# A convolution by FFT and a soft mixture of experts on one core: first stage in 60 and 30 columns, last stage in 64 and 26 frequencies, and the product in place

## The chip, the cores and the metric

The kernel runs on one NeuronCore of a Trainium2 chip. Its five engines are PE (matmul, with its weight loads shown as PEld), DVE (VectorE), ACT (ScalarE), POOL (GpSimd) and SP, whose queue issues nearly all DMAs here. Each runs its instructions in order. The metric is the device time of one execution in microseconds. All data are float32.

## The reference

```python
def _attn_ref(x, h):                     # x (8, 5696, 128), h (5696, 128)
    L = 2 * S
    Yf = np.fft.rfft(x, n=L, axis=1) * np.fft.rfft(h, n=L, axis=0)[None, :, :]
    return np.fft.irfft(Yf, n=L, axis=1)[:, :S, :]

def _moe_ref(x, phi, w1, w2):            # x (45568, 128), phi (128, 32)
    logits = x @ phi
    d = softmax over the 45568 tokens of logits
    slot_input = (d.T @ x).reshape(8, 4, 128)
    for e in range(8):
        slot_out[e] = np.maximum(slot_input[e] @ w1[e], 0) @ w2[e]   # 128 -> 1024 -> 128
    c = softmax over the 32 slots of logits
    return c @ slot_out                  # (45568, 128)
```

A causal convolution of every sequence with h along the tokens, then a soft mixture over all tokens, which weighs them over the whole batch before the experts can run.

## The kernel before, in words

The transform of a sequence is cut in two: 5,696 tokens are 89 rows of 64 (`N1` = 90 frequencies of the first stage, `N2` = 64 columns n2). It works on nine groups g: g = 0 is h, g = 1 to 8 are the sequences. The rows are mirrored, so sums and differences of two mirrored columns (`fold`, with `comp` 0 and 1) are transformed apart.

- **Stage A**, `stage_a(c, comp)`, one chunk c of 4 + 4 columns per step. `load_x` brings the rows (80 and 9 in two DMAs) into one of three tiles xc. `fold` adds or subtracts the mirrored half on POOL (L201) into xf[0] or xf[1]. Two matmuls by the 128-wide table s1 (L212, real and imaginary part) fill two PSUM banks, ACT copies them into fst (L214), and two DMAs of 45 partitions store them to f in DRAM (L218). The table has its 90 frequencies at columns 6 to 50 and 82 to 126.
- **Stage B**, for each unit u of up to eight frequencies, twelve units per group: `load_g` reads f (L236), `stage_b1` transforms over n2 with 64x64 matmuls into bt in PSUM (L250). DVE multiplies bt by Hr into pr and by Hi into pi (L270), and pr and pi are added and subtracted into yf (L279). The sum is on POOL where `share` is set, which is in steps with t < 27 or t >= 72. For g = 0 the same lines make Hr and Hi (L274, one half on POOL). `stage_b2` transforms back (L294), ACT copies bz to zst (L299), and one DMA stores z (L302).
- **Stage C**, for each of 32 pairs T of chunks: `load_pair` reads z (64 and 26 frequencies in two DMAs, L330) into the one tile zc. `stage_c1` makes four products by i1, each of two 64-column matmuls over 128 partitions (L349): two, then `stage_c4` of an earlier pair, then two more. ACT copies one of each two (L358, L362), DVE adds and subtracts (L354, L355). `after()` then folds the result out into y with four operations on POOL (L368). `stage_c2` transposes y (L377), ACT copies to yt (L379), `stage_c3` makes the logits (L386), `column_max` and `stage_c4` to `stage_c6`, `softmax` and `dispatch` do the softmaxes, the weighted sums over tokens and the storing of the combine weights.

PSUM is a ring of four banks for stages A and C, which `bank()` gives out in turn, and one buffer each for bt and bz.

The order is written out by hand: the pools run under `manual_schedule`, so every engine keeps the order of the program, and the kernel waits only for data and buffers. One loop over steps t places all stages. In step t it does, in this order: `stage_a(t, 0)`; `fold(t+1, 0)`; for even t `dispatch`; a unit of stage B in even t; in odd t `stage_c1` with `stage_c4` inside, in even t `stage_c2` and `stage_c6`; `after()`; in odd t a unit of stage B; `load_pair`; `load_x(t+3)`; in odd t `stage_c5`; `stage_a(t, 1)`; `fold(t+1, 1)`; in even t `stage_c3` and a second unit of stage B; `column_max` and `softmax`. Stage B starts in step 9, stage C in step 27, stage A ends with step 71, and the loop with step 80. So two steps, odd and even, are a period with three units of stage B and one pair of stage C. Behind the loop come the last pairs of stage C, the experts, and the combine with its stores to the output.

Of the kernel before, what the change touches and what calls it, by code (L numbers as in the profile page):

```python
# [10 lines left out]
F32 = mybir.dt.float32  # L11
AF = mybir.ActivationFunctionType
AL = mybir.AluOpType
# [4 lines left out]
def z_blocks(n):  # L18

    return [(0, 64, 32), (64, n - 64, 0)]  # L20


def transform_tables(S, N1, N2, CH, X0, F0, F1):

# [14 lines left out]
    s1 = np.stack([np.cos(a1), -np.sin(a1), -np.cos(a1)], 1)  # L41
    a0 = np.outer(alpha, np.arange(N1 // 2) + 0.5)
    i1 = np.stack([np.cos(a0), -np.sin(a0), -np.cos(a0)], 1)
    NP = N1 // 2
    part = s1
    s1 = np.zeros((P, 3, P))
    for a, p in enumerate((F0, F1)):
        s1[X0:X0 + R1, :, p:p + NP] = part[:, :, a * NP:(a + 1) * NP]
    part = i1[np.arange(N1).reshape(2, NP).T.reshape(-1)]
    i1 = np.zeros((P, 3, N2))  # L50
    for r, n, p in z_blocks(N1):
        i1[p:p + n, :, 0:NP] = part[r:r + n]
# [5 lines left out]
    back = np.arange(N2).reshape(2, HALF // CH, CH).transpose(1, 0, 2).reshape(-1)  # L58
# [5 lines left out]
    for a in range(2):  # L64
        wq[a] = w[a * NP:(a + 1) * NP].transpose(1, 0, 2)
        for q in range(NP):
            vq[q % 2, :, q // 2, a] = w[a * NP + q][back].T
            tn[q % 2, :, 0, q // 4, a, q // 2 % 2] = np.cos(turn[a * NP + q]) / N
            tn[q % 2, :, 1, q // 4, a, q // 2 % 2] = np.sin(turn[a * NP + q]) / N
    wq, vq, tn = [t.reshape(P, *t.shape[2:]) for t in (wq, vq, tn)]  # L70
    return [np.ascontiguousarray(t, dtype=np.float32) for t in (s1, i1, wq, vq, tn)]
# [3 lines left out]
def kernel(  # L75
# [42 lines left out]
    assert S == R1 * N2 and R1 == N1 - 1 and D == P and CH == Q == 4  # L118
    SPLIT = R1 // 16 * 16
    X0, F0, F1 = 20, 6, 82  # L120
    ctx.enter_context(tc.manual_schedule())

    t_s1, t_i1, t_w, t_v, t_turn = [
        nc.inline_tensor(t, f"tab_{n}").ap()
        for n, t in zip(("s1", "i1", "w", "v", "turn"), transform_tables(S, N1, N2, CH, X0, F0, F1))]
    fd = [nc.dram_tensor(f"f_{g}", (2, N2, NP, 2, D), F32, kind="Internal").ap() for g in range(B + 1)]
    zd = [nc.dram_tensor(f"z_{b}", (NP, 2 * N2, 2, D), F32, kind="Internal").ap() for b in range(B)]
# [8 lines left out]
    i1 = const.tile([P, 3, HP], F32, name="i1")  # L136
# [24 lines left out]
    s1 = apool.tile([P, 3, P], F32, name="s1", tag="s1", bufs=1)  # L161
# [12 lines left out]
    xf = [apool.tile([P, CH, D], F32, name=f"x{i}", tag=f"x{i}", bufs=1) for i in range(2)]  # L174
# [4 lines left out]
    def load_x(c):  # L179
        if c >= (B + 1) * NJ:  # L180
            return
        g, j = divmod(c, NJ)
        src = (h if g == 0 else x[g - 1]).rearrange("(a n) d -> a n d", n=N2)
        t_ = xcs[c % len(xcs)]
        gap = N2 - CH * (2 * j + 1)
        for r in (slice(0, SPLIT), slice(SPLIT, R1)):
            v = src[r, CH * j:CH * (j + 1), :]
            v = bass.AP(tensor=v.tensor, offset=v.offset,
                        ap=[v.ap[0], [gap * D, 2], [1, CH * D]])
            nc.sync.dma_start(  # L190
                out=t_[X0 + r.start:X0 + r.stop, :, :, :].rearrange("p s n d -> p s (n d)"), in_=v)
        xs[c] = t_
# [3 lines left out]
    def fold(c, comp):  # L196
# [3 lines left out]
        y_ = xf[comp]  # L200
        nc.gpsimd.tensor_tensor(out=y_[:, :, :], in0=t_[:, 0, :, :], in1=t_[:, 1, ::-1, :],  # L201
                                op=AL.subtract if comp else AL.add)
        folded[(c, comp)] = y_

    def stage_a(c, comp):
        g, j = divmod(c, NJ)
        src = folded.pop((c, comp))
        tab = (0, 1) if comp == 0 else (1, 2)
        st = apool.tile([P, CH, 2, D], F32, name="fst", tag="fst", bufs=5)
        for G in range(2):  # L210
            p = bank()
            nc.tensor.matmul(p[:, :], s1[:, tab[G], :],  # L212
                             src[:, :, :].rearrange("p n d -> p (n d)"), start=True, stop=True)
            nc.scalar.activation(st[:, :, G, :],  # L214
                                 p[:, :].rearrange("p (n d) -> p n d", d=D), AF.Copy)
        n0 = comp * HALF + CH * j
        for a, p in enumerate((F0, F1)):
            nc.sync.dma_start(  # L218
                out=fd[g][a, n0:n0 + CH, :, :, :].rearrange("n q c d -> q n (c d)"),
                in_=st[p:p + NP, :, :, :].rearrange("k n c d -> k n (c d)"))  # L220
# [9 lines left out]
    def load_g(u):  # L230
        if u >= (B + 1) * NW:
# [5 lines left out]
            out=t_[:, 0:n, :, :].rearrange("p q c d -> p (q c d)"),  # L237
            in_=fd[g].rearrange("a r q c d -> (a r) (q c d)")[:, 8 * w * D:(8 * w + 2 * n) * D])
        gs[u] = t_

    def stage_b1(u, share):
# [15 lines left out]
        else:  # L257
            pv = bt[r, :, 0, :].rearrange("p a (c d) -> p a c d", c=2)
        k = 2 * m
        tags = ("yf", "yf") if g == 0 and w % 2 else ("pr", "pi")  # L260
        pr, pi = [bpool.tile([P, 4, 2, D], F32, name="p", tag=x, bufs=2 if x == "yf" else 1)
                  for x in tags]
        for p_, H_ in ((pr, turn[:, 0]), (pi, turn[:, 1])) if g == 0 else ((pr, Hr), (pi, Hi)):
# [6 lines left out]
            nc.vector.tensor_tensor(out=p_[r, 0:k, :, :], in0=pv, in1=h_, op=AL.mult)  # L270
        if g == 0:
            for c, op_, H_, eng in ((0, AL.add, Hr, nc.vector), (1, AL.subtract, Hi, nc.gpsimd)):
                h_ = H_[r, w, :, :, :].rearrange("p a o d -> p (a o) d") if m == 2 else H_[r, w, :, 0, :]
                eng.tensor_tensor(out=h_, in0=pr[r, 0:k, c, :], in1=pi[r, 0:k, 1 - c, :], op=op_)  # L274
            return
        y_ = bpool.tile([P, 4, 2, D], F32, name="yf", tag="yf", bufs=2)
        for c, op_, eng in ((1, AL.add, nc.gpsimd if share else nc.vector),
                            (0, AL.subtract, nc.vector)):
            eng.tensor_tensor(out=y_[r, 0:k, c, :], in0=pr[r, 0:k, c, :],  # L279
                              in1=pi[r, 0:k, 1 - c, :], op=op_)  # L280
        prods[u] = y_

    def stage_b2(u):
# [6 lines left out]
        for o, (i, n) in enumerate(us):  # L290
# [11 lines left out]
        nc.sync.dma_start(  # L302
            out=zd[g - 1][4 * w:4 * w + k, :, :, :].rearrange("q r c d -> r q (c d)"),
            in_=st[:, :, :, :].rearrange("p o q x -> p (o q) x")[:, 0:k, :])
# [4 lines left out]
    zn = used = None  # L309
    ybufs = [ypool.tile([P, Q * CH, D + 1], F32, name=f"y{i}") for i in range(2)]  # L310
    zring = [ypool.tile([P, 2, 2, CH, 2, D], F32, name="zc")]
# [4 lines left out]
    nc.vector.memset(zring[0][:, :, :, :, :, :], 0.0)  # L316
# [5 lines left out]
    def load_pair(T):  # L322
# [5 lines left out]
        w_ = 2 * 2 * CH * 2 * D  # L328
        for r, n, p in z_blocks(N1):
            nc.sync.dma_start(  # L330
                out=t_[p:p + n, :, :, :, :, :].rearrange("k h o n c d -> k (h o n c d)"),
                in_=zd[b].rearrange("q (a r) c d -> (q a) (r c d)",
                                    a=2)[r:r + n, j * w_:(j + 1) * w_])
        zs[T] = t_

    def stage_c1(T, between):
        t_ = zs.pop(T)
        kr = used if t_ is zn else P
# [7 lines left out]
        def product(o, tab, q):  # L346
            p = bank()
            for h_ in range(2):
                nc.tensor.matmul(p[h_ * HP:(h_ + 1) * HP, :], i1[0:kr, tab, :],  # L349
                                 t_[0:kr, h_, o, :, q, :], start=True, stop=True)  # L350
            return p[:, :].rearrange("p (n d) -> p n d", d=D)

# [4 lines left out]
        b_, a_ = product(0, 1, 1), product(0, 0, 0)  # L357
        nc.scalar.activation(part(0, 0), b_, AF.Copy)  # L358
        fold_out(a_, part(0, 0), part(1, 0))
# [506 lines left out]
```

## Time and profile before

| | |
|---|---|
| device time, three runs | 924.53 us median (923.91 to 933.71) |
| span of the profiled execution | 922.1 us, from the first to the last instruction |
| PE, DVE, ACT, POOL busy | 818.0, 653.1, 481.7, 488.1 us |
| DMA | 272.45 MB in 156,552 packets, 295 GB/s over the span |
| mean granted PE clock | 0.943 |

Busy time is the time in which at least one instruction of an engine runs; matmuls are pipelined, so neighbours overlap. L12 is line 12 of the kernel that was profiled. An arrow in a wait names what released it. The profiled execution's own time outside the span is not recorded; the median stands 2.4 us above the span.

### The profile page before, as it was taken

Reading aid. Unit: us, or ns where it says so; the run is one execution under the profiler, and the core shown is the slowest. Engines: PE = TensorE matmul, PEld = TensorE weight load, DVE = VectorE, ACT = ScalarE, POOL = GpSimd, SP = SyncE. Lnnn points to the kernel's source line nnn. Section 1 sums busy time; section 2 is a strip of 40 time slices with the busy share of each in tenths; the row PEclk is TensorE's granted clock in tenths of the full one; section 3 lists DMA queues with packets and bytes.
Section 4 is the critical chain, followed back from the end, with each engine's and each line's share of the span. In section 5 each row is a group of like instructions: output and inputs, shape, how many; then the busy total and the mean of one; then the engine's idle time right before and its main releaser. Section 6 shows DMA issues by size and latency. Waiting matters only on the chain.

```text
span 922.1 us, 19325 instructions
## 1 busy us (share of the span) xinstructions
PE 818.0 (89%) x7220; PEld 423.9 (46%) x7220; DVE 653.1 (71%) x887; ACT 481.7 (52%) x888; POOL 488.1 (53%) x426
## 2 busy tenths in 40 slices
PE   6968898899999999999999999999987777878893
PEld 2323344345444445544554454444444434345783
DVE  3047665478888878888888788988887775674552
ACT  4623454455556655555666666656553344475442
POOL 4648766546655565556565655655466552472000
PEclk9989999899999999999999999999999888798865
DMA  9989999999899999999999999999989887761798
GB/s 298 279 274 299 272 345 311 289 345 327 268 320 319 314 282 324 316 314 285 341 304 327 289 324 329 297 318 320 316 269 330 272 254 198 211 249 73 272 405 341
DMA packets 156552, 272.45 MB, mean 295 GB/s; under 512 B 11766, under 2 KB 114422, under 8 KB 153317
## 3 DMA queue, kind: packets, MB, share of 16 engines
q1 hardware_dynamic: 155883, 270.85, 91.4%
q8 instruction: 58, 0.95, 0.4%
q10 hardware_dynamic: 576, 0.36, 0.2%
q14 instruction: 35, 0.29, 0.1%
HBM read 142.86 MB, written 128.21 MB: 294 GB/s over the span
## 4 chain that ended last, share of the span: by engine, by line
PE 51%; DMA 31%; POOL 5%; DVE 5%; issue 3%; SPq 2%; ACT 2%; DVEq 0%; POOLq 0%; ACTq 0%
PE bank L212 17%; DMA zc<-z 11%; PE bank L349 9%; DMA gt<-f 8%; PE bt L250 7%; PE bz L294 6%; DMA out_dram<-o 4%; PE bank L377 4%; DVE p L270 2%; POOL y L368 2%; DMA f<-fst 2%; PE bank L462 2%; DMA z<-zst 2%; PE bank L438 2%; PE bank L386 2%
## 5 line engine op out<-in xcount | busy, mean ns | idle before, releaser
L212 PE MATMUL bank<-x,s 128*128 128x512 f32 x576 | 275.9, 614 | 12.3 <-POOL x L201 12.0
L201 POOL TENSOR_TENSOR x<-xc 128x512 f32<-128x512 f32 x144 | 192.8, 1342 | 154.7 <-PE bank L212 70.4
L214 ACT ACTIVATE fst<-bank 128x512 f32<-128x512 f32 x288 | 171.9, 597 | 95.5 <-PE bank L212 74.8
L299 ACT ACTIVATE zst<-bz 128x1024 f32<-128x1024 f32 x96 | 93.2, 971 | 205.4 <-PE bz L294 198.5
L270 DVE TENSOR_TENSOR p<-bt,Hr 128x1024 f32<-128x1024 f32 x96 | 112.9, 1176 | 108.0 <-PE bt L250 95.7
L212 PEld LDWEIGHTS bank<-x,s 128*128 128x128 f32 x576 | 102.4, 193 | 131.5 <-issue 93.4
L279 DVE TENSOR_TENSOR yf<-p 128x512 f32<-128x512 f32 (+1 forms) x163 | 146.4, 931 | 3.3
L250 PE MATMUL bt<-gt,wt 64*64 64x256 f32 x1620 | 116.4, 394 | 25.1 <-DMA gt<-f 22.0
L349 PE MATMUL bank<-zc,i 128*64 128x512 f32 x480 | 117.1, 610 | 7.0 <-DMA zc<-z 4.1
L294 PE MATMUL bz<-yf,vt 64*64 64x256 f32 x1440 | 104.9, 393 | 15.5 <-POOL yf L279 15.0
L270 DVE TENSOR_TENSOR p<-bt,Hi 128x1024 f32<-128x1024 f32 x96 | 112.3, 1170 | 0.0
L250 PEld LDWEIGHTS bt<-gt,wt 64*64 64x64 f32 x1620 | 55.0, 134 | 102.0 <-issue 31.6
L368 POOL TENSOR_TENSOR y<-y,op 128x512 f32<-128x512 f32 x64 | 77.5, 1211 | 7.8 <-DVE op L354 5.1
L294 PEld LDWEIGHTS bz<-yf,vt 64*64 64x64 f32 x1440 | 58.2, 137 | 44.2 <-POOL yf L279 21.0
L279 POOL TENSOR_TENSOR yf<-p 128x512 f32<-128x512 f32 (+1 forms) x29 | 45.9, 1583 | 53.9 <-DVE p L270 53.9
L368 POOL TENSOR_TENSOR y<-y,om 128x512 f32<-128x512 f32 x54 | 71.8, 1330 | 2.1
L270 DVE TENSOR_TENSOR p<-bt,turn 128x1024 f32<-128x1024 f32 (+1 forms) x24 | 27.2, 1174 | 57.8 <-PE bt L250 57.7
L349 PEld LDWEIGHTS bank<-zc,i 128*64 128x64 f32 x480 | 30.8, 138 | 68.3 <-issue 40.8
L377 PE MATMUL bank<-ident,y 109*128 109x109 f32 x512 | 60.0, 275 | 0.7 <-DVE y L368 0.7
L377 PEld LDWEIGHTS bank<-ident,y 109*128 109x128 f32 x512 | 53.5, 151 | 13.6 <-issue 11.9
L379 ACT ACTIVATE yt<-bank 128x360 f32<-128x360 f32 x128 | 50.9, 482 | 3.3 <-PE bank L377 3.3
L819 PE MATMUL op<-so,cT 32*128 32x128 f32 x704 | 46.0, 374 | 4.4 <-ACT o L828 3.6
(97 smaller groups left out, 851.5 us busy)
## 6 DMA issues: line engine op xcount, KB each, us to landing
f<-fst SPq DMA_DIRECT2D x288, 180.0 KB
gt<-f SPq DMA_DIRECT2D x99, 512.0 KB
z<-zst SPq DMA_DIRECT2D x88, 512.0 KB
zc<-z SPq DMA_DIRECT2D x30, 1024.0 KB
xc<-in_x_dram SPq DMA_DIRECT2D x64, 320.0 KB
out_dram<-o SPq DMA_DIRECT2D x16, 1024.0 KB
zc<-z SPq DMA_DIRECT2D x30, 416.0 KB
out_dram<-o SPq DMA_DIRECT2D x8, 768.0 KB
```

The source lines that it names most:

```text
L201: nc.gpsimd.tensor_tensor(out=y_[:, :, :], in0=t_[:, 0, :, :], in1=t_[:, 1, ::-1, :], op=AL.subtract if comp else AL.add)
L212: nc.tensor.matmul(p[:, :], s1[:, tab[G], :], src[:, :, :].rearrange("p n d -> p (n d)"), start=True, stop=True)
L214: nc.scalar.activation(st[:, :, G, :], p[:, :].rearrange("p (n d) -> p n d", d=D), AF.Copy)
L250: nc.tensor.matmul(bt[q * HP:(q + 1) * HP, a, o, :], wt[r, 2 * i + q, :], t_[r, 2 * o + q, :, :].rearrange("p c d -> p (c d)"), start=True ...
L270: nc.vector.tensor_tensor(out=p_[r, 0:k, :, :], in0=pv, in1=h_, op=AL.mult)
L279: eng.tensor_tensor(out=y_[r, 0:k, c, :], in0=pr[r, 0:k, c, :], in1=pi[r, 0:k, 1 - c, :], op=op_)
L294: nc.tensor.matmul(bz[a * HP:(a + 1) * HP, q, o, :], vt[r, i, a, :], y_[r, a * m + o, :, :].rearrange("p c d -> p (c d)"), start=True, sto ...
L299: nc.scalar.activation(st[:, 0:m, 0:n, :].rearrange("p o q x -> p q o x"), bz[:, 0:n, 0:m, :], AF.Copy)
L349: nc.tensor.matmul(p[h_ * HP:(h_ + 1) * HP, :], i1[0:kr, tab, :], t_[0:kr, h_, o, :, q, :], start=True, stop=True)
L368: eng.tensor_tensor(out=part_, in0=part(v, 0), in1=o_[:, :, :], op=sign)
L377: nc.tensor.transpose(p[:, i * TR:(i + 1) * TR], ys[T][0:TR, k * CH + i, 0:D], ident[0:TR, 0:TR])
L379: nc.scalar.activation(yt[:, k * CH:(k + 1) * CH, :, :], of_tokens(p), AF.Copy)
```

## The change

- **Stage A.** Both folds of a chunk now stand in one tile, xf is three such tiles, and `stage_a(c, high)` is split by frequency, not by fold. In every step `stage_a(t, False)` makes frequencies 0 to 59 of both folds of chunk t, two 64-column matmuls side by side in each bank. In odd steps, in the place of the former second call, `stage_a(t, True)` makes frequencies 60 to 89 of both folds of chunks t-1 and t, four 32-column matmuls in each bank. There are three evictions per step on average, not four. f is stored frequency by frequency, so a store is one run of 4 KB per partition (60 partitions, or 30), and `load_g` reads runs of 1 KB.
- **The nine last rows** of a load go to partitions 100, 103, ..., 124, not to 100 to 108.
- **Product in place.** Hi's product goes to pi, Hr's back into bt itself; sum and difference read bt and pi, both on DVE; `share` is gone.
- **z.** Its rows are split by the half o of n2, which alternate on the partitions of zst. Frequencies 0 to 63 go to zm by two DMAs, 64 to 89 to zr by four, with real and imaginary part apart (512-byte runs). zr has two buffers, whose padding is zeroed at the start by eight DMAs on ACT's queue.
- **Stage C.** `load_pair` reads zm and zr, 128 partitions each. `stage_c1` makes all four products first: eight 64x64 matmuls over 64 frequencies and eight 32x64 matmuls over 26, which accumulate in four banks. `stage_c4` follows.

The core of the diff (the tables follow it and are left out):

```diff
+        for r, p in ((slice(0, SPLIT), slice(X0, X0 + SPLIT)), (slice(SPLIT, R1), slice(X1, X1 + XSTEP * (R1 - SPLIT - 1) + 1, XSTEP))):
...
-        y_ = xf[comp]
+        y_ = xf[c % len(xf)]
...
+    def stage_a(c, high):
+        st = apool.tile([P, CH, 2, D], F32, name="fst", tag="fst", bufs=4)
+        if high:
+            groups = [(c_, o, HALF, slice(HP, HP + HALF)) for c_ in (c - 1, c) for o in range(2)]
+        else:
+            groups = [(c, o, HP, slice(0, HP)) for o in range(2)]
+        for q in range(2):
+            p = bank()
+            for i, (c_, o, m, cols) in enumerate(groups):
+                nc.tensor.matmul(p[i * m:(i + 1) * m, :], s1[:, q + o, cols], columns(c_, o),
+                                 start=True, stop=True)
             nc.scalar.activation(...)
+        k0, k1 = (LOW, N1) if high else (0, LOW)
+        for i, (c_, o, m, _) in enumerate(groups):
+            n0 = o * HALF + CH * (c_ % NJ)
+            nc.sync.dma_start(
+                out=fd[g][k0:k1, n0:n0 + CH, :, :].rearrange("k n c d -> k (n c d)"),
+                in_=st[i * m:i * m + k1 - k0, :, :, :].rearrange("k n c d -> k (n c d)"))
...
-        for p_, H_ in ((pr, turn[:, 0]), (pi, turn[:, 1])) if g == 0 else ((pr, Hr), (pi, Hi)):
+        for p_, H_ in (((pi[r, 0:k, :, :], turn[:, 1]), (pv, turn[:, 0])) if g == 0 else
+                       ((pi[r, 0:k, :, :], Hi), (pv, Hr))):
...
-        for c, op_, eng in ((1, AL.add, nc.gpsimd if share else nc.vector),
-                            (0, AL.subtract, nc.vector)):
+        for c, op_ in ((1, AL.add), (0, AL.subtract)):
+            nc.vector.tensor_tensor(out=y_[r, 0:k, c, :], in0=pv[:, :, c, :],
+                                    in1=pi[r, 0:k, 1 - c, :], op=op_)
...
+        for o in range(2):
+            if 8 * w < MAIN:
+                nc.sync.dma_start(
+                    out=zm[g - 1][o, 8 * w:8 * w + 2 * k].rearrange("(q a) r c d -> (a r) q (c d)", a=2),
+                    in_=sv[o::2, 0:k, :])
+                continue
+            k0 = 8 * w - MAIN
+            for c in range(2):
+                nc.sync.dma_start(
+                    out=zr[g % 2][o, c, k0:k0 + 2 * k].rearrange("(q a) r d -> (a r) q d", a=2),
+                    in_=sv[o::2, 0:k, c * D:(c + 1) * D])
...
+        ps = {(o, c): bank() for o, c in ((0, 1), (1, 0), (0, 0), (1, 1))}
+        for c in (1, 0):
+            for h_ in range(2):
+                for o in range(2):
+                    r = slice(o * HP, (o + 1) * HP)
+                    nc.tensor.matmul(ps[o, c][h_ * HP:(h_ + 1) * HP, :], im[r, c, :],
+                                     zt[r, h_, :, c, :], start=True, stop=False)
+        for h_ in range(2):
+            for (o, c), p in ps.items():
+                r = slice((2 * o + c) * HALF, (2 * o + c) * HALF + N1 - MAIN)
+                nc.tensor.matmul(p[h_ * HP:(h_ + 1) * HP, :], ir[r, :], zx[r, h_, :, :],
+                                 start=False, stop=True)
...
-            stage_a(t, 0)
+            stage_a(t, False)
             fold(t + 1, 0)
...
-            stage_a(t, 1)
+            if t % 2:
+                stage_a(t, True)
             fold(t + 1, 1)
```

## The prediction, made before the changed kernel ran

> **What bounds the kernel now.** I read the busy line first, then the stretches, then the timeline of one pair of steps, then the waits. PE is busy for 89% of the span and the SP queue's packets fill 91% of the 16 DMA engines, so both look full:
>
> ```profile
> PE 818.0 (89%) x7220; PEld 423.9 (46%) x7220; DVE 653.1 (71%) x887; ACT 481.7 (52%) x888; POOL 488.1 (53%) x426
> q1 hardware_dynamic: 155883, 270.85, 91.4%
> ```
>
> An average hides the stages. By stretches (columns: stretch; busy us and count of PE, PEld, DVE, ACT, POOL; granted clock; DMA share; GB/s), the first is steps 0 to 26, before any last-stage work; the second the 22 pairs of steps in which all stages run, from the first `stage_c1` at 182.6 us to the one at 664.7; the third the four pairs after the first stage has ended:
>
> ```profile
> 0.00:182.60 182.60, 149.15 (x841) 62.85 (x841) 87.21 (x89) 79.61 (x124) 114.92 (x90) 0.96 0.94 295
> 182.60:664.70 482.10, 469.80 (x4146) 234.99 (x4145) 407.14 (x542) 286.70 (x521) 277.02 (x240) 1.00 0.99 313
> 664.70:743.20 78.50, 64.87 (x700) 35.22 (x700) 60.07 (x87) 34.76 (x65) 43.49 (x38) 0.93 0.91 293
> ```
>
> A pair takes 482.1 / 22 = 21.9 us and PE is busy for 97% of it: PE's own work sets the pace, with the DMA engines just as full beside it. The first stretch is DMA's (share 0.94, PE 82%).
>
> The timeline of one pair shows what matters for this change, POOL against PE (columns: start, us, engine, line, operation, count):
>
> ```profile
> 474.07 2.44 POOL L368 TENSOR_TENSOR y<-y,op 128x512 f32<-128x512 f32 x2
> 476.48 2.76 POOL L368 TENSOR_TENSOR y<-y,om 128x512 f32<-128x512 f32 x2
> 479.20 1.71 POOL L201 TENSOR_TENSOR x<-xc 128x512 f32<-128x512 f32 x1
> ...
> 475.42 3.60 PE L212 MATMUL bank<-x,s 128*128 128x512 f32 x8
> 478.95 1.09 PE L462 MATMUL bank<-y,d 128*32 128x129 f32 x32
> ```
>
> The eight passes at 475.42 are the second half of `stage_a` of odd step t and then the first half of step t+1, which starts at 477.14. POOL's `fold(t+1, 1)` runs behind the four L368 operations of `after()` and ends at 480.91, 3.8 us after PE has begun step t+1. Today that costs nothing, since only `stage_a(t+1, 1)`, at 483.89, reads it. The same lateness stands in the other pairs (3.7 to 5.0 us in those from 477 to 654).
>
> **The change, part by part.**
>
> *First stage on PE.* An f32 matmul is two passes. A full-width pass of 512 costs 275.9 us / 576 = 479 ns (L212), a 64-column pass 117.1 / 480 = 244 ns (L349), a 32-column pass 3.64 / 32 = 114 ns (L764). A pair had 16 full passes, 7.7 us. Now the 60 columns take 8 passes of 64 columns in each step (1.95 us) and the 30 columns of both steps 16 passes of 32 columns in the odd step (1.8 us): 5.7 us, a saving of 1.9. ACT's L214 drops from 8 to 6 evictions of 597 ns; nothing waits there.
>
> *Last stage on PE.* `stage_c1` had 16 passes of 244 ns, 3.9 us. Now 16 passes on 64x64 tiles, priced by L250 (16 passes of 256 columns in 0.92 us from start to start, so 1.85 us for 512), and 16 on 32x64 tiles, which no row shows: 0.95 us if eight run at once, 1.85 if four. L819 packs four row groups at 40 ns a pass, near its share, so I take 0.95: 2.8 in all, a saving of 1.1. The Trainium skill (TensorE: Matmul & The Clock Gate, Measured speedup vs the span model) has four row tiles of 512 gain 3.07 rather than 4; by that the 0.95 would be 1.25 and the total 6 us longer. L250's fourfold packing shows no such loss: 58 ns a pass, where a quarter of a full-width pass of 256 columns is 60. The four banks are now taken at once; the two that `stage_a` used last come free by L214, 0.85 us after its end, while the first half of c1 runs.
>
> *In-place product.* Two operations on PSUM at the price of L354 (0.69 us) replace L279 (0.93 mean on DVE, stretched to 1.6 when POOL runs). Where POOL did one of them (L279, 29 times, and L274), DVE now does both. A unit costs DVE 2 x 1.18 + 2 x 0.69 = 3.75 us, three units 11.2, with the rest 18 us per pair. bt is held 1.4 us longer; its next writer comes 4 us later, so nothing waits, unless DVE starts late.
>
> *The new wait.* `stage_a(t+1, False)` reads both folds of step t+1, as the first thing PE does in that step. For odd t the second fold stands on POOL, in the order of the changed program's instructions, behind L431 and the four L368, and PE's second matmul of the step waits for it. Behind that matmul wait all of the step's PE work and then DVE and ACT. I lay out one pair from the end of odd `stage_a`:
> - To the fold: c1 2.8; copy of y with its signal 0.7 (L358, 0.60), since c4's bank is freed by it and all four products now come first; c4 0.7; copy of L 0.65; DVE rm 0.75; POOL L431 with the memset before it 1.35; four L368 at 1.2, the price without DVE beside it, 4.8; fold 1.27, signal 0.1. Sum 13.1.
> - PE's own work meanwhile: c1 2.8, wait for y 0.8, c4 0.6, b1 and b2 1.9, c5 0.5, the 32-column matmuls 1.9. Sum 8.5. PE stands still for 4.6 us, less 1.0 for the step's first matmul, which needs only the first fold.
> - After the fold: `stage_a` 1.9, dispatch 1.0, b1 and b2 1.9, c2 1.6, c6 0.45, wait for yt 0.15, c3 0.75, b1 and b2 1.9, `stage_a` 1.9. Sum 11.55.
>
> A pair: 13.1 + 11.55 = 24.65 us against 21.9, +2.75, over 22 pairs +60 us. The 3.0 us that PE saves is smaller than the 4.6 + 0.8 of new waits.
>
> *The clock.* PE will stand for 3.6 us in each pair. In the third stretch it stands for 2.84 us before L294, and what follows runs at half speed:
>
> ```profile
> 480.89 1.04 PE L294 MATMUL bz<-yf,vt 64*64 64x256 f32 x16
> 715.04 1.98 PE L294 MATMUL bz<-yf,vt 64*64 64x256 f32 x16 [2.84 <-POOL yf L279]
> ```
>
> The clock there is 0.93 over 78.5 us, 5.5 us lost in four pairs, 1.4 each; in the second stretch 1.00. Bounds: 0, as after the shorter waits of the second stretch, to 1.7 in every pair (L294 and the L377 after it lost 0.9 and 0.8). I take 0.85: +19 us. The skill (same page, HAM oscillation) says that a gap longer than its 3.4 us window re-throttles each turn; by it the term would be 37, and it speaks against this change.
>
> *DMA.* The f stores go from 1,024-byte packets to 4,096, the gt loads the other way, 26 of 90 z rows to 512 bytes. In the trace's packet records 1,024 bytes take 46 ns (median) and 4,096 take 159, so f gains what gt loses. z becomes 3 to 8 DMAs per pair, 5 more SP issues of 0.4 us, and `load_pair` moves 1,536 KB, not 1,440, on all 128 partitions. A pair's 6.8 MB in 24.65 us is 276 GB/s, against 313 reached now, so in the second stretch I cost it at nothing; the cover is PE's longer pair, and gone below 276 GB/s. In steps 0 to 26, 27 x 180 f packets of 4,096 gain 25 ns each (4 x 46 - 159) on 16 engines, 7.6 us, the 27 gt loads of 128 such packets lose 5.4, and steps 0 to 8, now 4.0 us apart (L212 at 31.65, 35.76 and 39.76), of which PE 3.7, may gain 0.5 each: -6 us (bounds -15, +8: the 1 KB loads may stretch as the 4 KB ones do, 203 mean to 159 median, and the eight new zero-fills on ACT's queue may hold its first evictions).
>
> *After step 71.* POOL's L279 leaves the chain (it delayed L294 above), but DVE's 18 us then sets a pair of 19.6: about 18.6, -4 us (0 to -6). Then: `stage_c1` is shorter, the first load needs no copy of a gap: -4 (-8 to +3).
>
> **Sum.** 922.1 - 6 + 60 + 19 - 4 - 4 = 987. The median of the runs is 924.53, 2.4 above this span: 989.
>
> **Rivals.**
> - *The fold stays hidden (faster).* One mechanism: the POOL chain from c1 to the fold takes 8.5 us or less, not 13.1, so PE keeps its saving, at 18.9 us a pair, until DMA stops it: 6.7 MB at the best stretch's 321 GB/s is 20.9. 22 x -1.0, and -14 elsewhere: 922 - 36 + 2 = 888. It decides from a chain 2.75 us shorter than I sum (there a pair is as now). For it: POOL is only 53% busy and loses L279. Against: in every pair read the fold is 3.7 us late or more, and nothing moves it ahead of L368.
> - *The gain and the wait cancel (no change).* The chain is 2 to 3 us shorter through a free DVE: 925. Against: only 0.5 us of L368 and 0.45 of the fold are stretched by DVE now, and these are out of my sum.
> - *DMA becomes the bound (slower).* If 1 KB loads and 512-byte stores pull the rate to 250 GB/s, a pair takes 27.2 us: +116, and +10 in the first stretch: 1050. It decides below 276 GB/s. For it: the engines are full now; against: the bytes are the same within 1%.
>
> **How the numbers follow.** The fold wait 0.75 (its own range 950 to 1025: the chain's terms to half a us either way, the clock 0 to 37), fold hidden 0.12, cancelled 0.06, DMA 0.07. A measurement of this kernel tells about 1% from no change. Faster by over 1% 0.12, within 1% 0.06, slower 0.82. The range 930 to 1040 leaves out the hidden fold and half of the DMA case.
>
> **What would show it.** PE's second `stage_a` matmul of even steps waiting for POOL's fold, some 3.6 us, 22 times; pairs of 25 us; PE near 73% and a clock near 0.97 in that stretch, DMA share under 0.95 there; the 32x64 group near 1 us; no POOL wait before b2. The forecast is wrong if pairs are below 22 us, or if PE waits there for DMA instead.

## The result, and the profile after

The changed kernel takes 1,025.89 us (median of four runs, 1,018.48 to 1,029.66), the kernel before 929.12 us beside it (923.91 to 935.97): a ratio of 1.104, with a 95% interval of 1.095 to 1.112. The profiled execution took 1,018.48 us, 1.8 more than its span of 1,016.7; it is the shortest of the four and has the highest mean granted clock (0.911, the others 0.894 to 0.897), so what is read from it below stands 7.4 us under the median.

The page's busy lines and the SP queue's line show that neither of the two full resources is full now:

```profile
PE 788.5 (78%) x8308; PEld 386.1 (38%) x8308; DVE 631.6 (62%) x928; ACT 440.9 (43%) x816; POOL 401.1 (39%) x385
q1 hardware_dynamic: 176287, 273.91, 83.2%
```

The same stretches as before, cut at the first matmul of the same calls of `stage_c1` (columns: stretch; busy us and count of PE, PEld, DVE, ACT, POOL; granted clock; DMA share; GB/s):

```profile
0.00:197.10 197.10, 136.91 (x1052) 49.54 (x1052) 99.23 (x116) 62.84 (x96) 70.38 (x63) 0.90 0.89 274
197.10:771.10 574.00, 467.90 (x4850) 213.00 (x4848) 366.80 (x540) 262.71 (x476) 256.61 (x239) 0.94 0.86 271
771.10:847.50 76.40, 60.50 (x778) 35.55 (x780) 63.99 (x99) 35.01 (x66) 27.39 (x28) 0.93 0.88 289
847.50:1016.70 169.20, 123.22 (x1636) 88.04 (x1628) 101.54 (x176) 80.36 (x178) 46.72 (x55) 0.81 0.71 265
```

The 22 pairs, 482.1 us before, are 574.0: a pair has gone from 21.9 to 26.1 us, +91.9 of the +94.6 in all. Steps 0 to 26 cost 14.5 us more (182.6 before), the four pairs behind step 71 2.1 less, the rest 9.7 less. In the pairs PE has gone from 97% to 82% busy and the DMA share from 0.99 to 0.86: both now wait for something else.

One pair shows it, PE first (columns: start, us, engine, line, operation, tiles, count, and the idle time before with its releaser), then POOL:

```profile
535.08 1.95 PE L374 MATMUL bank<-zc,im 64*64 64x512 f32 x16
536.96 1.11 PE L379 MATMUL bank<-zx,ir 26*64 26x512 f32 x16
...
541.83 2.93 PE L218 MATMUL bank<-x,s 128*32 128x512 f32 x18
548.14 1.93 PE L218 MATMUL bank<-x,s 128*64 128x512 f32 x6 [3.38 <-POOL x L200]
...
560.08 1.95 PE L374 MATMUL bank<-zc,im 64*64 64x512 f32 x16
```

```profile
542.03 2.46 POOL L392 TENSOR_TENSOR y<-y,op 128x512 f32<-128x512 f32 x2
544.44 2.43 POOL L392 TENSOR_TENSOR y<-y,om 128x512 f32<-128x512 f32 x2
546.84 1.25 POOL L200 TENSOR_TENSOR x<-xc 128x512 f32<-128x512 f32 x1
```

PE has done two passes of the even step's `stage_a` and then stands for 3.38 us until 548.14, when POOL's fold (L200) has ended at 548.09 behind the four operations of `after()` (now L392). The waits of PE over all 22 pairs have this as their first line (columns: us in total, times, longest):

```profile
PE bank L218 <- POOL x L200: 72.6, 21, 4.1
PE bank L439 <- ACT y L382: 14.9, 21, 0.7
```

### The profile page after: what moved, and what is told of

It reads as the page before. It is cut to its first block, busy times and chain, and to the rows that moved or that the text cites. A ratio compares the mean times of both kernels' runs of the same rounds, so it can differ in the third digit from the quotient of the medians.

```text
span 1016.7 us, 21393 instructions
## 1 busy us (share of the span) xinstructions
PE 788.5 (78%) x8308; PEld 386.1 (38%) x8308; DVE 631.6 (62%) x928; ACT 440.9 (43%) x816; POOL 401.1 (39%) x385
## 3 DMA queue, kind: packets, MB, share of 16 engines
q8 instruction: 65, 1.06, 0.4%
## 4 chain that ended last, share of the span: by engine, by line
PE 48%; POOL 15%; DMA 13%; ACT 9%; DVE 6%; issue 6%; SPq 2%; POOLq 0%; DVEq 0%; ACTq 0%
PE bank L218 15%; POOL y L392 9%; PE bt L260 9%; PE bz L303 6%; PE bank L374 5%; DMA gt<-f 4%; DMA out_dram<-o 4%; PE bank L486 4%; ACT yt L403 4%; PE bank L379 3%; POOL x L200 3%; ACT zst L308 3%; PE bank L410 2%; POOL L L455 2%; ACT y L382 2%
## 5 line engine op out<-in xcount | busy, mean ns | idle before, releaser
L218 PE MATMUL bank<-x,s 128*32 128x512 f32 (+1 forms) x1152 | 259.9, 654 | 91.5 <-POOL x L200 91.4
L200 POOL TENSOR_TENSOR x<-xc 128x512 f32<-128x512 f32 x144 | 180.3, 1268 | 178.7 <-PE bank L218 88.0
L220 ACT ACTIVATE fst<-bank 128x512 f32<-128x512 f32 x216 | 128.8, 597 | 214.0 <-PE bank L218 181.0
L280 DVE TENSOR_TENSOR pi<-bt,Hi 128x1024 f32<-128x1024 f32 x96 | 112.9, 1176 | 92.6 <-PE bt L260 92.6
L218 PEld LDWEIGHTS bank<-x,s 128*32 128x32 f32 (+1 forms) x1152 | 59.4, 129 | 246.5 <-POOL x L200 121.7
L288 DVE TENSOR_TENSOR yf<-bt,pi 128x512 f32<-128x512 f32 x192 | 119.3, 662 | 3.3
L280 DVE TENSOR_TENSOR bt<-bt,Hr 128x1024 f32<-128x1024 f32 x96 | 113.0, 1177 | 0.0
L303 PE MATMUL bz<-yf,vt 64*64 64x256 f32 x1440 | 108.2, 398 | 0.0
L392 POOL TENSOR_TENSOR y<-y,op 128x512 f32<-128x512 f32 x64 | 77.6, 1212 | 5.4 <-DVE op L366 2.9
L491 DVE SCALAR_TENSOR_TENSOR acc<-acc,dn,bank 128x129 f32<-128x129 f32 x31 | 10.1, 326 | 106.6 <-PE bank L486 106.6
L303 PEld LDWEIGHTS bz<-yf,vt 64*64 64x64 f32 x1440 | 63.1, 141 | 24.1 <-issue 2.2
L392 POOL TENSOR_TENSOR y<-y,om 128x512 f32<-128x512 f32 x54 | 63.7, 1180 | 2.1
L374 PE MATMUL bank<-zc,im 64*64 64x512 f32 x480 | 58.4, 600 | 0.0
L401 PEld LDWEIGHTS bank<-ident,y 109*128 109x128 f32 x512 | 51.9, 148 | 13.1 <-issue 11.0
L280 DVE TENSOR_TENSOR pi<-bt,turn 128x1024 f32<-128x1024 f32 (+1 forms) x12 | 14.1, 1176 | 66.7 <-PE bt L260 66.6
```

What stands on the lines that cost most here:

```text
L200: nc.gpsimd.tensor_tensor(out=y_[:, comp, :, :], in0=t_[:, 0, :, :], in1=t_[:, 1, ::-1, :], op=AL.subtract if comp else AL.add)
L218: nc.tensor.matmul(p[i * m:(i + 1) * m, :], s1[:, q + o, cols], columns(c_, o), start=True, stop=True)
L220: nc.scalar.activation(st[:, :, q, :], p[:, :].rearrange("p (n d) -> p n d", d=D), AF.Copy)
L280: nc.vector.tensor_tensor(out=p_, in0=pv, in1=h_, op=AL.mult)
L288: nc.vector.tensor_tensor(out=y_[r, 0:k, c, :], in0=pv[:, :, c, :], in1=pi[r, 0:k, 1 - c, :], op=op_)
L303: nc.tensor.matmul(bz[a * HP:(a + 1) * HP, q, o, :], vt[r, i, a, :], y_[r, a * m + o, :, :].rearrange("p c d -> p (c d)"), start=True, sto ...
```

## The experiments

The stretches of all profiled kernels, us. Each row is one execution, and kernels that are alike up to step 26, or nearly, differ there by up to 7 us (196.3 and 203.1 with the fold early and with no zr loads, 205.7 and 198.4 in the rows with the x load first throughout and with 26 rows of zr, which has no zero-fills), so a smaller difference in the first column says nothing by itself:

| kernel | steps 0 to 26 | a pair (of 22) | four pairs | rest | span |
|---|---|---|---|---|---|
| before | 182.6 | 21.91 | 78.5 | 178.9 | 922.1 |
| after | 197.1 | 26.09 | 76.4 | 169.2 | 1016.7 |
| after, fold early | 196.3 | 22.15 | 78.7 | 169.6 | 931.9 |
| after, two operations on DVE | 199.3 | 23.59 | 91.6 | 177.7 | 987.5 |
| after, full-width first stage | 189.9 | 22.43 | 75.9 | 172.4 | 931.6 |
| before, first stage alone | 223.3 | 25.60 | 77.5 | 182.0 | 1046.0 |
| the same, fold early | 192.5 | 22.09 | 79.7 | 180.9 | 939.1 |
| before, product in place alone | 188.7 | 22.05 | 71.0 | 182.4 | 927.2 |
| fold early, no zr loads | 203.1 | 20.95 | 77.9 | 169.6 | 911.5 |
| fold early, zero-fills late | 198.6 | 22.41 | 78.9 | 168.9 | 939.4 |
| the same, x load first | 205.7 | 21.76 | 76.4 | 171.1 | 931.8 |
| the same, x load first from step 27 | 200.3 | 21.78 | 76.5 | 168.8 | 924.7 |
| x load first, 26 rows of zr | 198.4 | 23.54 | 78.0 | 169.1 | 963.4 |
| zero-fills late, f stores on ACT | 203.6 | 24.47 | 77.4 | 168.7 | 988.1 |

### The fold moved ahead of after()

```diff
             stage_a(t, False)
             fold(t + 1, 0)
+            fold(t + 1, 1)
...
                 stage_a(t, True)
-            fold(t + 1, 1)
```

> The changed kernel with one line moved: fold(t+1, 1) is issued right after fold(t+1, 0), so on POOL it stands ahead of the memset, the subtraction and the four operations of after(). Theory (the fold's place on POOL's queue makes the new wait): PE no longer waits for POOL in even steps, a pair falls from 26.1 us to about 21.2 (PE's own work of the prediction, 8.5 + 11.55 = 20.05 us, held back a little by DMA: 6.8 MB at the 321 GB/s of the best stretch), the clock returns to 0.98 or more; 1,017 - 22 x 4.9 = 909 us, range 895 to 930. Rival (the new packets and the added DMAs set the pair): PE's wait moves to gt or to the f stores and the time stays above 1,000. Rival in between: the next wait is POOL's end of after() before dispatch or DVE, 940 to 980.

It took 937.69 us, a ratio to before of 1.010 (1.006 to 1.014): one line gives back nearly all of the loss, though the time lies above the expected range. The pair is 22.15 us. PE's waits for the fold are gone from the 22 pairs; what is new in their place is DMA. The stretch's row, and the first lines of POOL's and PE's waits in it:

```profile
196.30:683.60 487.30, 436.05 (x4854) 211.37 (x4852) 375.35 (x539) 260.96 (x476) 258.64 (x239) 0.96 0.96 316
```

```profile
POOL x L200 <- DMA xc<-in_x_dram: 124.1, 21, 12.3
```

```profile
PE bank L439 <- ACT y L382: 14.9, 21, 0.7
PE bt L260 <- DMA gt<-f: 14.7, 10, 5.1
```

POOL now waits for its input to land, PE for gt, and the DMA share is 0.96. The theory holds for the wait. It was too hopeful by 1 us a pair on what would come next: 316 GB/s, not 321, and 316 x 22.15 us = 7.0 MB, not 6.8; and the granted clock came back to 0.96 only, not to 0.98.

### The chain made shorter, the fold left late

```diff
-            for v, o_, eng in ((1, op, nc.gpsimd), (0, om, nc.vector if tail else nc.gpsimd)):
+            for v, o_, eng in ((1, op, nc.gpsimd), (0, om, nc.vector)):
```

> The changed kernel with two of the four operations of after() (those with om) on DVE instead of POOL, in all steps. Theory (POOL's chain from c1 to the fold sets the pair): the chain is 2.4 us shorter (two of 1.2), so the pair falls from 26.1 to about 23.5, more where the clock recovers: 1,017 - 22 x 2.4 to 3.8 = 933 to 964 us, and PE's wait for the fold shrinks by 2 us but does not vanish. Rival (DMA or DVE sets the pair): no change, or a loss through 1.4 us more on DVE, 1,010 to 1,050.

The pair came out at 23.59 us, 2.5 less for two operations of 1.2, and PE's wait at 37.9 us over 21 times, 1.8 each in place of 3.46:

```profile
PE bank L218 <- POOL x L200: 37.9, 21, 2.2
```

So POOL's chain sets the pair, but the gain is not the chain alone: 1.6 of the 2.5 us are the shorter wait, and 0.8 are PE's busy time (467.9 us over the pairs before, 450.1 now, at a granted clock of 0.98 in place of 0.94). From the memset to the end of the fold POOL took 7.4 us in the pair shown above and takes 5.8 in one of this kernel (532.76 to 538.57), 1.6 less and not 2.4, because POOL's other operations are longer there (the fold 1.72 us, not 1.25). The total, 993.91 us (ratio 1.071, 1.064 to 1.078), missed the expected range by 30: the 55 us won in the pairs were partly lost behind step 71, where DVE now carries two more operations and the four pairs take 91.6 us, not 76.4, and the rest 8.5 more.

### The first stage alone in the kernel before

```diff
-    def stage_a(c, comp):
+    def stage_a(c, high):          # as in the change, with f by frequency
...
-            stage_a(t, 1)
+            if t % 2:
+                stage_a(t, True)
             fold(t + 1, 1)
```

> The kernel before with the first stage alone changed (60 and 30 columns, both folds in one tile, f by frequency, stage B's tables in that order); the product through pr and pi, z, and the last stage with its two halves around stage_c4 are as before, and the fold's place is that of the changed kernel. Theory: the wait comes with this part alone. POOL's chain starts earlier, because stage_c4 stands after the first two products: 1.95 + copies 1.35 + DVE to rm 1.35 + 1.35 + 4.8 + 1.37 = 11.9 us against PE's own 8.8, a pair of about 23.4, and with the clock 24.3: 922 + 22 x 2.4 - 3 = 972 us, range 950 to 1,000; PE waits some 2 us for POOL 22 times. Rival (the z stores, the last stage or the product cause the loss): the saving of 1.9 us of PE per pair shows, 890 to 915.

1,052.06 us, a ratio of 1.135 (1.128 to 1.143): the first stage alone costs more than the whole change. The pair is 25.60 us, where 24.3 was expected. The six pairs at a granted clock of 1.00 take 24.2 us on average, 0.8 more than the sum of the chain, and the others, at 0.87 to 0.93, bring the mean 1.4 higher, where 0.9 was allowed for. The total lies 52 us above the expected range. The larger part of that, which nobody expected, is in steps 0 to 26, 223.3 us. There the product's sum is still on POOL (L290), waits for DVE, and stands ahead of the fold; POOL's timeline and then PE's:

```profile
147.27 1.77 POOL L290 TENSOR_TENSOR yf<-p 128x512 f32<-128x512 f32 x1 [6.41 <-DVE p L281]
149.00 1.27 POOL L201 TENSOR_TENSOR x<-xc 128x512 f32<-128x512 f32 x1
```

```profile
139.69 3.56 PE L219 MATMUL bank<-x,s 128*64 128x512 f32 x6 [2.83 <-POOL x L201]
```

It is the same queue with another operation in front. PE's waits for the fold in these steps are 48.1 us in 17:

```profile
PE bank L219 <- POOL x L201: 48.1, 17, 8.2
```

In the full change this operation has left POOL; there they are 18.8 us in 5, and the stretch is 26 us shorter.

### The same with the fold early

```diff
             fold(t + 1, 0)
+            fold(t + 1, 1)
...
-            fold(t + 1, 1)
```

> The kernel before with the first stage alone changed, as in the run of that part, and in addition fold(t+1, 1) right after fold(t+1, 0). Theory (the same queue, with another operation ahead of the fold: in steps 9 to 26 POOL's sum of the product stands there and waits for DVE, in steps 27 to 71 the four operations of after()): the first stretch falls from 221.8 us to 195 or less, the pair from 25.5 us to about 21.7, the packet time of a pair of the kernel before, and the total to 925 to 940. Rival (the first stretch was long through something else in the first stage's layout, such as 1 KB runs in the gt loads): it stays above 210, and the total above 945.

942.75 us, 1.012 (1.005 to 1.019), a little above the expected range. Steps 0 to 26 fall from 223.3 to 192.5 us and the pair from 25.60 to 22.09. Both losses of the first stage are thus for the most part the place of the fold. What is left is 9.9 us in the first steps. PE's saving in the first stage buys nothing: the pair was 21.91 us before.

### The rest of the change, the first stage at full width

```diff
-    def stage_a(c, high):
+    def stage_a(c, o):             # one fold, all 90 columns in one pass of 96
...
+            nc.tensor.matmul(p[0:m, :], s1[:, q + o, :], columns(c, o), start=True, stop=True)
...
```

> The changed kernel with its first stage by folds again: full-width passes, stage_a(t, 0) reading only the first fold and stage_a(t, 1) in every step only the second; f, z, the product in place, the last stage and the zero-fills stay as changed. Theory: without the dependence on the second fold at the head of the step PE has no wait on POOL; PE's own pair is 20.05 + 1.9 = 22 us and the total 922 + 10 (start) + 0 to 10 = 920 to 945 us. Rival (something else in the change makes the pair long): above 980.

931.51 us, 1.003 (0.9995 to 1.006), the pair 22.43. The other parts of the change together move nothing in the total that can be measured; within it the pairs and the first steps are longer and the last stretch is shorter. The fold stands as late on POOL as in the changed kernel, but only `stage_a(t, 1)` reads it.

### What sets the pair once the wait is gone

```diff
+        if all(t_ is not k for k in loaded_zx):
+            loaded_zx.append(t_)
             nc.sync.dma_start(
                 out=t_[1][:, :, :, :].rearrange("p h n d -> p (h n d)"),
```

> The early fold, with the loads of zr (512 KB per pair) left out except for the first one of each tile, so that the last 26 frequencies of the later pairs are stale: a test of what sets the pairs. Theory (with the wait gone the DMA engines set the pair: their packets take 21.25 us of its 22.02): 128 packets of 4 KB at 190 ns on 16 engines are 1.5 us less, the pair falls to about 20.5, and the total by 22 x 1.5 = 33 us to 905. Rival (PE, or a chain of waits, sets the pair, and the full engines are only beside it): the pair stays near 22 and the total above 930.

910.87 us, 0.976 (0.970 to 0.982), where 905 was expected. The pair falls by 1.2 us to 20.95, toward PE's own 20.05, and the DMA share to 0.95 at 309 GB/s:

```profile
203.10:664.00 460.90, 424.26 (x4850) 203.77 (x4848) 365.09 (x539) 260.62 (x476) 258.89 (x239) 0.99 0.95 309
```

Taking bytes away shortens the pair, so with the fold early it is DMA that holds the mean pair above PE's own time. Of the 1.5 us of packets taken away 1.2 arrived.

How it does so shows pair by pair, and it is not an even pace. With the fold early 12 of the 22 pairs run at a granted clock of 1.00 and take 20.7 us on average (20.2 to 21.2); the other ten, at 0.86 to 0.93, take 23.9 (22.7 to 25.0). Nine of these ten hold a wait of PE of 1.35 us or more, four for gt and five for DVE; the 12 hold none above 1.06. Without the zr loads 19 pairs run at 1.00, at 20.5 us on average, and three below it. So only some 0.2 of the 1.2 us are shorter pairs at full clock; the rest is that there are fewer pairs in which PE stands and then runs slower. One of them with the fold early, the wait and the slower passes behind it, and the same passes (L303) of the next unit at 1.04 us:

```profile
289.60 1.09 PE L260 MATMUL bt<-gt,wt 64*64 64x256 f32 x16 [2.47 <-DMA gt<-f]
290.48 1.73 PE L303 MATMUL bz<-yf,vt 64*64 64x256 f32 x16
...
299.31 1.04 PE L303 MATMUL bz<-yf,vt 64*64 64x256 f32 x16
```

How much of such a pair is the wait and how much the clock was not separated.

### The zero-fills at another time

```diff
+        if NJ < t <= 2 * NJ:
+            i = t - NJ - 1
+            nc.scalar.dma_start(
+                out=zr[i // 4][i // 2 % 2, i % 2, N1 - MAIN:]...
...
```

> The early fold, and the eight zero-fills of zr moved from the start to the ends of steps 9 to 16 (one each, same queue). Theory (the zero-fills hold ACT's first evictions until 11.9 us and with them the first stores and the load of chunk 3): the folds of chunk 3 start some 4 us earlier, at about 20 us as in the run without zero-fills (19.93) and not at 24.5, and the total falls by 3 to 4 us, to about 934. Rival (the late start is made good again by step 26, since the gt loads set the order there): the first load comes earlier and the total stays within 1 us of 937.

941.03 us (1.009, 1.005 to 1.013), where the fold early alone had 937.69 (1.010). POOL's timelines, first of the kernel with the zero-fills at the start, then with them late, show that chunk 3 does come 4.8 us sooner:

```profile
24.55 4.93 POOL L200 TENSOR_TENSOR x<-xc 128x512 f32<-128x512 f32 x4 [10.29 <-DMA xc<-in_h_dram]
```

```profile
19.71 2.48 POOL L200 TENSOR_TENSOR x<-xc 128x512 f32<-128x512 f32 x2 [5.66 <-DMA xc<-in_h_dram]
```

By step 26 nothing of it is left (198.6 against 196.3 us). The ratio to before is the same, so the rival was right: the zero-fills are not the 14.5 us.

### The x load ahead of the stores

```diff
         if t < NA:
+            load_x(t + 3)
             stage_a(t, False)
...
-        if t < NA:
-            load_x(t + 3)
```

> The early fold, the late zero-fills, and load_x(t+3) at the head of step t, ahead of the f stores on SP's queue; its tile is free there, since both folds of chunk t are done. Theory (in the first 30 us the x load queues on SP behind stores that wait for both folds): the folds of chunk 3 start at about 16 us as before the change (15.6), another 3 to 4 us less in the first stretch; in the pairs nothing, since DMA's packets fill them: about 930. Rival (later x loads cost nothing, or earlier ones only push gt loads back): 932 to 940.

929.96 us, 0.997 (0.993 to 1.0005), 11 less than without it, but not where it was expected: steps 0 to 26 are no shorter (205.7, and 198.4 in the last run below, which has the same order there), and the pairs are, by 0.65 us (21.76, DMA at 323 GB/s). With the x loads first the DMA engines are better fed in the pairs (six of them are below full clock, nine without).

### The x load first only from step 27

```diff
+            if t >= LAG_C:
+                load_x(t + 3)
             stage_a(t, False)
...
-        if t < NA:
+        if t < min(NA, LAG_C):
             load_x(t + 3)
```

> The early fold and the late zero-fills, with load_x(t+3) at the head of the step only from step 27 on; before that it stands where the change has it. Theory (the two stretches are independent: x loads put first help the pairs, 21.76 us where they were 22.41, and cost the first stretch 7 us by pushing back gt loads): the sum of the better parts, 198.6 + 478.7 + 76.4 + 171.1 = 925 us of span beside 931.8, time about 923, ratio to the kernel before 0.990. Rival (the pairs gain only because the first stretch has loaded ahead, the sum of both is what DMA needs): 928 to 941 us, ratio 0.996 to 1.01.

925.67 us, 0.9956 (0.9919 to 0.9992), the best of the versions built on the change that load all of z, and 0.4% faster than the kernel before. The pairs keep 21.78 us, so their gain was not loaded ahead in the first steps. That the first steps gain by the old order is not shown: 200.3 against 205.7 and 198.4 is within the scatter. The pairs' row:

```profile
200.30:679.50 479.20, 431.01 (x4854) 207.27 (x4852) 363.55 (x541) 260.77 (x476) 257.77 (x239) 0.97 0.97 322
```

### The product in place alone

```diff
-        for p_, H_ in ((pr, turn[:, 0]), (pi, turn[:, 1])) if g == 0 else ((pr, Hr), (pi, Hi)):
+        for p_, H_ in (((pi[r, 0:k, :, :], turn[:, 1]), (pv, turn[:, 0])) if g == 0 else
+                       ((pi[r, 0:k, :, :], Hi), (pv, Hr))):
...
```

> The kernel before with the product in place alone: Hr's product back into bt, sum and difference on DVE from bt and pi, none on POOL. Theory, as predicted: nothing in the pairs, 0 to -3 us in the first stretch (POOL's sum no longer waits for DVE ahead of the folds), -4 us after step 71: about 926 beside 931, ratio 0.995. Rival (bt is held 1.4 us longer by DVE and stage B waits for it): the pair gets up to 1 us longer, 935 to 955.

926.98 us, 0.9963 (0.993 to 0.9998), as expected in total. The four pairs behind step 71, where POOL's sum stood in the chain, gain 7.5 us, more than the 4 that were expected. The +6.1 in steps 0 to 26 is no gain, but within the scatter, and the pairs are the same.

### Two that failed

The f stores on ACT's queue:

```diff
-            nc.sync.dma_start(
+            nc.scalar.dma_start(
                 out=fd[g][k0:k1, n0:n0 + CH, :, :].rearrange("k n c d -> k (n c d)"),
```

> The early fold, the late zero-fills, and the f stores issued on ACT's queue, right behind the evictions, in place of SP's. Theory (in steps 9 to 26 the chain runs through SP: matmuls of stage A, eviction, six store issues of 0.4 us, then the gt load of 5.3 us and stage B): the gt loads no longer stand behind the stores, the first stretch shrinks by about 10 us (196 to 186), the pairs stay at 22 us: about 924. Rival (ACT's issues delay its evictions as much, or the stretch is set by DMA): 930 to 945.

990.83 us, 1.062 (1.055 to 1.070): the rival named evictions that are delayed, but at 930 to 945 us it was far too small. ACT's timeline, and PE's waits in the pairs:

```profile
413.25 1.51 ACTq L225 DMA_DIRECT2D f<-fst  x2
414.81 1.02 ACT L308 ACTIVATE zst<-bz 128x1024 f32<-128x1024 f32 x1 [4.40 <-DMA f<-fst]
```

```profile
PE bank L510 <- ACT yt L403: 40.3, 20, 3.9
```

By the profile it is the landing of an f store that releases the copy of bz, which reads and writes neither f nor fst: the copy stands behind a store's issue in ACT's order, 4.40 us here. So yt comes late, and PE waits for yt 2 us in each pair. The first steps did not get shorter either (203.6), so the stores ahead of the gt loads on SP are not shown to be what lengthens them.

Four loads of 26 partitions in place of one of 128:

```diff
+        for k in range(4):
+            nc.sync.dma_start(
+                out=t_[1][k * HALF:k * HALF + N1 - MAIN, :, :, :].rearrange("p h n d -> p (h n d)"),
...
```

> The early fold and the x load first, and zr read by four loads of 26 partitions in place of one of 128, so that its padding is neither read nor zeroed. Theory (DMA's packets set the pair): 24 of 128 packets less per pair, 96 KB of 6.98 MB, 0.28 us of packet time, so 22 x 0.28 = 6 us less than with the x load first alone: 924 beside 931, ratio 0.992. Rival (26 packets spread unevenly over 16 engines, and three more issues on SP's queue cost as much): 928 to 936.

965.53 us, 1.039 (1.035 to 1.043), with 96 KB less per pair and a pair 1.8 us longer. By share and length of the pair the packets took 0.92 x 23.54 = 21.7 us, where the one load had 0.97 x 21.76 = 21.1, and PE waits 37.0 us for gt in the pairs, not 16.9; 15 pairs are below full clock, not six. First the four loads, then the one:

```profile
PE bt L260 <- DMA gt<-f: 37.0, 17, 5.6
```

```profile
PE bt L260 <- DMA gt<-f: 16.9, 8, 4.8
```

The Trainium skill (DMA: Bandwidth & Descriptors, Why a DMA increments its semaphore by 16 and not by 1) says that a DMA runs on the largest number of engines up to 16 that divides the slowest dimension of both its sides. By that, as an estimate, 26 partitions use 13 engines, four such loads put 8 packets on each of these, as many as the one load of 128 puts on all 16, and the busiest engines gain nothing. The profile keeps no engine numbers, so no run here shows it, and the three more issues on SP remain a second candidate.

## Why the prediction was right, point by point

- **The new wait: right.** Predicted 3.6 us on the second matmul of even steps, 22 times; measured 72.6 us in 21, 3.46 each. From the end of odd `stage_a` to the fold's end 13.1 us were laid out, and the pair shown has 548.09 - 535.08 = 13.0. Behind it 11.55 were laid out, and it has 560.08 - 548.14 = 11.9. Moving one line takes the wait away, and taking two of the four operations off POOL's chain cuts the wait to 1.8 us and the pair by 2.5.
- **First and last stage on PE: right in kind, the saving too large.** The 32x64 group takes 1.11 us with its end, predicted 0.95. The skill's 3.07-fold speedup, which gave 1.25, was a little too slow and the row of L250 a little too fast. The saving is 2.6 us a pair, not 3.0. `stage_c1` had 85.0 us of busy time in the 22 pairs and has 67.3 without the zr loads, where the clock is 0.99: 0.8 a pair for 1.1. The first stage had 166.0 and has 126.4: 1.8 for 1.9.
- **The clock: right mechanism, a little small.** Seven pairs ran at a granted clock of 1.00 and took 24.6 to 25.0 us, the one shown 25.0; the other 15 ran at 0.86 to 0.94, and the mean is 26.09. Put down to the clock, that is 1.09 a pair, 24 us, where 0.85 and 19 were taken. The skill's rule, by which every such gap throttles, gave 37. Of the signs that were named, two missed in size: PE is busy for 82% of the pairs, not 73, and the clock is 0.94, not 0.97.
- **DMA at nothing in the pairs: right, with the cover named.** The cover was PE's longer pair. With the fold early it is gone, and the mean pair is 22.15 us with packets in 0.96 of it. So the rival that hid the fold, 888 us, would have been 50 too low: over the mean of the pairs PE's saving is worth nothing. Of the 50, 27 are its 6.7 MB at 321 GB/s, where 7.0 MB moved at 316; most of the rest is the next point. The rival had no term for the clock, which falls in ten of these pairs.
- **Steps 0 to 26: wrong in sign.** The term said -6 (bounds -15 to +8), the runs +14.5. It was worked out from packet times, as if DMA still set this stretch; its share fell from 0.94 to 0.89, so packet times alone do not give its length. Of the two losses that the prediction named, the zero-fills are nothing by step 26, and longer 1 KB loads were not tried. Every kernel with a part of the change is longer there than the 182.6 us of before: 188.7 with the product in place alone, 192.5 with the first stage alone and the fold early, 189.9 with everything but the first stage's split. The sum is beyond the scatter (196.3 to 205.7 in the nine kernels with the whole change), its parts hardly are. For the product the step in doubt is "bt is held 1.4 us longer; its next writer comes 4 us later, so nothing waits": units that arrive late follow each other closely, and in this stretch PE waits 13.6 us for DVE to leave bt, in the kernel before not at all. These are all of PE's waits there in the kernel before that the profile lists, and then two of the changed kernel's:

```profile
PE bt L250 <- DMA gt<-f: 17.5, 9, 6.9
PE bank L212 <- POOL x L201: 12.0, 9, 8.2
PE bz L294 <- POOL yf L279: 3.7, 6, 1.0
```

```profile
PE bt L260 <- DVE yf L288: 9.0, 3, 3.0
...
PE bt L260 <- DVE Hi L284: 4.6, 1, 4.6
```

The prediction also put the clock at nothing in this stretch, and the granted clock fell there from 0.96 to 0.90. The same 24 passes of the first stage take 5.79 us behind a late unit and 3.79 later on:

```profile
74.77 5.79 PE L218 MATMUL bank<-x,s 128*32 128x512 f32 x24
...
134.67 3.79 PE L218 MATMUL bank<-x,s 128*32 128x512 f32 x24
```

The part of the stretch that the clock withheld goes from 0.04 x 182.6 = 7 us to 0.10 x 197.1 = 20, an estimate of 12 us more if all of it lay on the path. The length goes with the clock in the other kernels too: 188.7 and 189.9 us at 0.96 in the two with a full-width first stage, 192.5 at 0.91, 196.3 to 205.7 at 0.90 to 0.87 in the nine; only the first stage alone with its late fold (223.3 at 0.91) stands outside. Whether the clock makes the stretch long or the waits make both was not tried, so how the 14.5 us divide stays open.

- **After step 71: right in sum.** -4 and -4 were predicted, -2.1 and -9.7 measured. The last stretch is as long as before or longer with the product in place alone (182.4 us) and with the first stage alone (182.0 and 180.9), and shorter with everything but the first stage's split (172.4), so its gain goes with z and the last stage. In the four pairs the product alone gains 7.5 us; what takes 5.4 of them back was not tried.
- **The sum.** Against 987 the span is 1,016.7: +20.5 from the first steps, +12.9 from the pairs (91.9, not 79: 0.35 us a pair of chain, 0.24 of clock), +1.9 and -5.7 from the last two stretches. The median of the runs, 1,025.89, is another 7.4 above this execution, at a lower granted clock, and 37 above the 989 that were forecast.

## What to carry to other kernels

When an operation is made to read two inputs where it read one, ask for each engine's queue where the later input is produced, and what stands ahead of it: here a fold that had been 3.8 us late for nobody became the pace of the loop, and one line moved on POOL was worth 88 us. Two resources that are both full must be relieved together: some 2.6 us of PE in each pair were saved and the mean pair did not get shorter, since DMA's packets took 21 of 22 us, and where data came late PE stood and its clock fell. The same queue punishes a late operand wherever it stands: with the sum of the product still on POOL, the first steps lost 31 us to it as well (223.3 to 192.5).

## What the runs showed of the hardware

The clock does not follow the length of the last wait alone. After a wait of 3.38 us the same six passes ran at full speed (1.93 us, shown above), after one of 3.39 at little more than half of it, and after one of 3.81 at half; another wait of 3.39, at 418.42, was followed by 1.93 us:

```profile
337.94 3.29 PE L218 MATMUL bank<-x,s 128*64 128x512 f32 x6 [3.39 <-POOL x L200]
```

```profile
390.74 3.68 PE L218 MATMUL bank<-x,s 128*64 128x512 f32 x6 [3.81 <-POOL x L200]
```

The Trainium skill (TensorE: Matmul & The Clock Gate, HAM oscillation) gives as a rule that PE should have no idle gaps above about 3.4 us. These runs show lower clocks after shorter waits too: 2.84 us before L294 in the kernel before, 2.83 in the first stage alone (both shown above), and in that kernel two waits of the same 2.88 us were followed by 1.93 us for the six passes at 362.48 and by 3.67 at 485.35. For a wait of 2.8 to 3.4 us the price is therefore between nothing and a doubled group, and a bound from both sides is the most that can be said.
